# Splitting weight pieces with the low part one tile later, and re-spacing the copy, read-back and product of the DMA-transposed attention tiles

## Chip, cores and metric

One core of one Trainium2 chip runs the program. The metric is the device time of one launch in microseconds (us). The chip draws TensorE's clock from a gate: the profile gives the granted clock of a stretch as a share of full speed.

## What is computed

An attention with a mask by hashing, then a mixture of four experts, all in float32:

```python
q_bits = einsum("bhsd,dk->bhsk", q, proj) > 0        # likewise k_bits; b=2, h=8, s=768, d=64, k=6
mask = q_bucket[:, :, :, None] == k_bucket[:, :, None, :]
scores = where(mask, scale * q @ k.T, -1e9)
attn = softmax(scores) @ v                           # per batch and head
x = attn, heads side by side                         # (1536, 512)
p = domain_probs / (domain_probs.sum(-1) + 1e-9)
out = sum over e of p[:, e] * (relu(x @ w1[e]) @ w2[e])   # w1 (4, 512, 1024), w2 (4, 1024, 512)
```

## The kernel before

**Arithmetic.** Matmuls are made of rounded operands in pairs: a high part (the rounded value) and a low part (the rest), and three products (high·high, high·low, low·high) stand for one float32 product. Each operand needs a copy that rounds it (ScalarE or VectorE) and a subtraction that gives the low part (VectorE or GpSimd).

**Three stages.** First comes the attention of batch 0. Then the experts of batch 0 run interleaved with the attention of batch 1. Last come the experts of batch 1 in another form (`moe_fast`), without attention beside them. A loop at the end of the file mixes two Python generators: `moe` gives one tile of matmuls after another, and `attention` is advanced whenever its estimated cost has fallen behind the experts' by the ratio `ATT_PACE * n_att / n_moe`. Everything is written in program order, and each engine executes its own instructions in that order; nothing reorders them.

**Attention.** The work is a sequence of steps, one for each tile of 128 queries by 768 keys (six to a head). A step `i` runs the operations of `ORDER`, letter by letter, each for the tile that lies its lag behind: S, the scores (four matmuls `sps`, and their minimum on VectorE); E, the exponential on ScalarE; N and R, the row sums, which go to DRAM and come back broadcast; P, the preparation of the next head (`prep_head`), the split of v and loads. The softmax weights must then be transposed. In the first nine heads TensorE does it (T). In the last seven heads of batch 1 (`light`) it goes by DMA, two tiles (a group) at a time: X transposes blocks of 32 by 32 on VectorE and writes them to DRAM (`scr`), Y reads them back in another order (four DMAs into `ptlo`), H rounds them on ScalarE (`pthi`, line 450) and takes the low part on GpSimd (`ptlo`, line 451), V multiplies both by v (`pv`, line 461): six matmuls that read `pthi` (part 0), then six that read `ptlo` (part 1), and ScalarE and VectorE add the halves up (`xtmp`, `xraw`). There are 21 such groups. Before, both parts of V follow each other at once in the step eight behind.

**Experts.** A unit has eight tiles of the first layer (`mps`, lines 677 to 679, twelve matmuls of 384 columns; ScalarE writes `hh`, VectorE `hl`) and six of the second (lines 640 to 642, twelve matmuls of 512 columns; VectorE adds to `acc`). Weights come in loads of two pieces (`ws`, line 602, two buffers). `split_w` yields once a piece: VectorE casts the high part (line 613), GpSimd takes the low part (line 614), and behind every second piece the next load is issued. One `yield` is used up behind each tile of the layer before the one that needs the weights, and in the first stage behind every `W_STEP`-th attention operation.

**Queues.** All DMAs are issued by SyncE, in program order. A load of `ws` that waits for a buffer holds back all DMAs that are written behind it.

Of the kernel before, what the change touches and what calls it, by code (L numbers as in the profile page):

```python
# [31 lines left out]
WC = 2  # L32
N_WARM = 16
WARM = (2, 4)
FIRST = 2
W_STEP = 24
PREP_AT = 0
ORDER = "TXVSENRPHY"
LIGHT_FROM = 9
LAG_VL = 8  # L40
DRAIN = 1000
LAG_X = 3
LAG_Y = 4
# [4 lines left out]
def tile_lsh_attention__then__domain_moe(  # L48
# [206 lines left out]
    def prep_head(b, h):  # L255
        tqk = loaded.pop((0, b, h))
        q1, al, ah, k2 = stack_tiles(b, h)
        ps = big("tps")
        for c in range(NT):
            nc.tensor.transpose(  # L260
                ps[:, c // 3, (c % 3) * P : (c % 3 + 1) * P], tqk[:, c].rearrange("p a d -> p (a d)"), ident
            )
        src = ps[:, :, :NH]
        nc.scalar.activation(two(ah), src, ACTF.Copy, scale=qk_scale)
        nc.vector.scalar_tensor_tensor(
            out=two(al), in0=src, scalar=qk_scale, in1=two(ah.bitcast(F32)), op0=ALU.mult, op1=ALU.subtract
        )
        nc.sync.dma_start(out=q1[0:D].bitcast(F32), in_=ah[0:D].bitcast(F32))
        nc.sync.dma_start(out=q1[D:P].bitcast(F32), in_=ah[0:D].bitcast(F32))
        nc.sync.dma_start(out=k2[0:D].bitcast(F32), in_=ah[D:P].bitcast(F32))  # L270
        yield 654
        ps = big("hps")
        for j, (w, a) in enumerate(((phi, ah), (plo, ah), (phi, al))):
            for i in range(2):
                sl = slice(i * NH, (i + 1) * NH)
                nc.tensor.matmul(ps[:MKE, i, :NH], w, a[:, sl], start=j == 0, stop=j == 2)
        nc.sync.dma_start(out=ah[0:D].bitcast(F32), in_=al[D:P].bitcast(F32))
        nc.scalar.activation(
            two(k2[D:MKE]), ps[D:MKE, :, :NH], ACTF.Sign, bias=sgn_bias[D:MKE], scale=SGN_SCALE
        )  # L280
        yield 978
        nc.gpsimd.tensor_scalar(
            out=al[D:MKE],
            in0=k2[D:MKE].bitcast(F32),
            scalar1=1.0,
            scalar2=bit_mul[D:MKE],
            op0=ALU.add,
            op1=ALU.mult,
        )
        nc.sync.dma_start(out=k2[MQ:MQE].bitcast(F32), in_=al[MK:MKE].bitcast(F32))  # L290
        yield 0
# [218 lines left out]
    def attention():  # L510
        n = len(seq)
        prep = [iter(())]

        def stage_light(f, j):
            if 0 <= j < n and light(*seq[j][:2]) and j % G == G - 1:
                b, h, t = seq[j]
                f(b, h, t // G)

        def do(op, i):
            if op == "N":  # L520
                j = i - LAG_N
                if 0 <= j < n and j % G == G - 1:
                    b, h, t = seq[j]
                    stage_n(b, h, t // G)
            elif op == "R":
                j = i - LAG_R
                if 0 <= j < n and j % G == G - 1:
                    b, h, t = seq[j]
                    stage_r(b, h, t // G)
            elif op == "T":  # L530
                j = i - LAG_T
                if 0 <= j < n and not light(*seq[j][:2]):
                    stage_t(*seq[j])
                    return 654
            elif op == "X":
                stage_light(stage_x, i - LAG_X)
            elif op == "H":
                stage_light(stage_h, i - LAG_H)
            elif op == "Y":
                stage_light(stage_y, i - LAG_Y)  # L540
            elif op == "S":
                if i < n:
                    b, h, t = seq[i]
                    if t == 0:
                        x = hseq.index((b, h))
                        prep[0] = prep_head(*hseq[x + 1]) if x + 1 < len(hseq) else iter(())
                    stage_s(b, h, t)
                    return 652
                return DRAIN
            elif op == "V":  # L550
                c = None
                for il, lag in enumerate((LAG_V, LAG_VL)):
                    for part in range(G):
                        j = i - lag - part * (not il)
                        if 0 <= j < n and j % G == G - 1 and light(*seq[j][:2]) == bool(il):
                            b, h, t = seq[j]
                            stage_v(b, h, t // G, part)
                            if part == G - 1 and h == H - 1 and t == NT - 1:
                                done_b[b] = True
                            c = 654 + (c or 0)  # L560
                return c
            elif op == "E":
                j = i - LAG_E
                if 0 <= j < n:
                    stage_e(*seq[j])
            elif op == "P":
                if i < n:
                    b, h, t = seq[i]
                    c = next(prep[0], None) if t >= PREP_AT else None
                    x = hseq.index((b, h))  # L570
                    if t == QK_AT and x + 2 < len(hseq):
                        load_qk(*hseq[x + 2])
                    if t == 4:
                        split_v(b, h)
                        if x + 2 < len(hseq):
                            load_v(*hseq[x + 2])
                    return c
            return None

        for i in range(n + max(LAG_V, LAG_VL) + G + 1):  # L580
            for op in ORDER:
                c = do(op, i)
                if c is not None:
                    yield c
# [20 lines left out]
    def split_w(g, i):  # L605
        n = ("w1", "w2")[i]
        hi = wp.tile([P, KD, HALF], F32R, tag=n + "hi", name=n + "hi")
        lo = wp.tile([P, KD, HALF], F32R, tag=n + "lo", name=n + "lo")
        wts[g, i] = (hi, lo)
        for c in range(0, KD, WC):  # L610
            t = staged.pop((g, i, c))
            for o in range(WC):
                nc.vector.tensor_copy(hi[:, c + o], t[:, o])  # L613
                nc.gpsimd.tensor_tensor(  # L614
                    out=lo[:, c + o], in0=t[:, o], in1=hi[:, c + o].bitcast(F32), op=ALU.subtract
                )
                if o == WC - 1:
                    load_w()
                yield

    accs = {}

# [37 lines left out]
    def moe(b, first_u):  # L660
        for u in range(NU):
            w1hi, w1lo = wts.pop((first_u + u, 0))
            sp2 = split_w(first_u + u, 1) if first_u + u else iter(())
            hs = {}
            nxt = first_u + u + 1
            xo = None
            for s in range(NS):
                if nxt == NU and s == 1:
                    while next(att, None) is not None:
                        pass  # L670
                    xo = x_ops()
                sl = slice(s * SB, (s + 1) * SB)
                for f in range(FC):
                    fs = slice(f * P, (f + 1) * P)
                    ps = moe_ps()
                    for kk in range(KD):
                        nc.tensor.matmul(ps[:, :SB], w1hi[:, kk, fs], xhi[b, kk][:, sl], start=kk == 0, stop=False)  # L677
                        nc.tensor.matmul(ps[:, :SB], w1hi[:, kk, fs], xlo[b, kk][:, sl], start=False, stop=False)  # L678
                        nc.tensor.matmul(  # L679
                            ps[:, :SB], w1lo[:, kk, fs], xhi[b, kk][:, sl], start=False, stop=kk == KD - 1  # L680
                        )
                    hh = hp.tile([P, SB], F32R, tag=f"hh{f}", name="hh")
                    hl = hp.tile([P, SB], F32R, tag=f"hl{f}", name="hl")
                    nc.scalar.activation(hh, ps[:, :SB], ACTF.Relu)  # L684
                    nc.vector.scalar_tensor_tensor(  # L685
                        out=hl, in0=ps[:, :SB], scalar=0.0, in1=hh.bitcast(F32), op0=ALU.max, op1=ALU.subtract
                    )
                    hs[s, f] = (hh, hl)
                    if s == 0:
                        next(sp2, 0)  # L690
                    yield 1960
                    if xo is not None and (s, f) >= (1, 1):
                        next(xo, 0)
            for _ in xo or ():
                pass
            yield from second_layer(b, u, first_u, hs, wts.pop((first_u + u, 1)))

# [257 lines left out]
```

## Time and profile before

| | before |
|---|---|
| time, median of 3 runs | 810.42 us (810.42 to 812.13) |
| time of the profiled execution | 812.0 us |
| its span (first to last instruction) | 810.3 us |
| mean granted TensorE clock | 0.971 |
| busy in the span: TensorE, VectorE, ScalarE, GpSimd | 756.5, 506.2, 362.3, 339.1 us |
| DMA moved, mean rate | 95.49 MB, 118 GB/s |

TensorE is busy for 93% of the span. The first stage ends near 160 us, the DMA-transposed groups run from about 205 to 492 us, and the experts of batch 1 begin near 555 us. The profile is read by asking where in these stages TensorE stands still or is slow, and which instruction it then waits for.

### The profile page before, as it was taken

What the parts mean: (1) busy time and instruction counts of PE and PEld (TensorE: products, weight loads), DVE (VectorE), ACT (ScalarE), POOL (GpSimd) and SP (SyncE); (2) the same over time, 40 slices, a digit from 0 to 9 for tenths busy, and PEclk for the clock granted to TensorE, in tenths of its full rate; (3) what the DMA queues carried; (4) which work ended last, traced back from release to release, by engine and by line L of the source; (5) the groups of instructions that cost most, each with busy time, mean ns of one, the idle gap of its engine ahead of it and who ended that gap; (6) DMA issues with size and microseconds to landing.
All of it is one profiled execution on the core that took longest, in us unless ns stands there. A gap on an engine that the chain in (4) does not pass through costs nothing. (4 is left out here: it accounts for less than half of the span.)

```text
span 810.3 us, 11425 instructions
## 1 busy us (share of the span) xinstructions
PE 756.5 (93%) x4090; PEld 684.9 (85%) x4090; DVE 506.2 (62%) x957; ACT 362.3 (45%) x731; POOL 339.1 (42%) x290
## 2 busy tenths in 40 slices
PE   7899999999889899998887888999999999999998
PEld 6889889998878879888777777888899898898896
DVE  4899999755546447474555322378765756756753
ACT  4999999643434334433434211043343343433430
POOL 1232532613555446465446343375443433423520
PEclk8999999999999899999999798999999999999999
DMA  3545535425756755875276321114211211302202
GB/s 95 148 111 126 118 98 150 128 62 178 202 172 167 229 153 161 231 216 183 81 215 201 120 69 53 52 53 157 78 53 59 98 53 53 104 28 77 83 23 78
DMA packets 71953, 95.49 MB, mean 118 GB/s; under 512 B 31396, under 2 KB 47268, under 8 KB 71896
## 3 DMA queue, kind: packets, MB, share of 16 engines
q1 hardware_dynamic: 71896, 94.76, 39.9%
q8 instruction: 32, 0.52, 0.3%
q14 instruction: 25, 0.20, 0.1%
HBM read 62.68 MB, written 19.71 MB: 102 GB/s over the span
## 5 line engine op out<-in xcount | busy, mean ns | idle before, releaser
L640 PE MATMUL mps<-w2hi,hh 128*128 128x512 f32 x384 | 153.7, 400 | 0.6 <-DVE acc L648 0.4
L642 PE MATMUL mps<-w2hi,hl 128*128 128x512 f32 x384 | 153.1, 399 | 0.0
L641 PE MATMUL mps<-w2lo,hh 128*128 128x512 f32 x384 | 152.7, 398 | 0.0
L648 DVE SCALAR_TENSOR_TENSOR acc<-mps,pe,acc 128x512 f32<-128x512 f32 x84 | 62.9, 748 | 90.2 <-PE mps L642 88.8
L365 ACT ACTIVATE p<-p,nb 128x768 f32<-128x768 f32 x96 | 89.5, 932 | 14.0 <-DVE p L349 13.3
L816 POOL TENSOR_TENSOR w2lo<-ws,w2hi 128x512 fp32r<-128x512 f32 x32 | 45.8, 1452 | 114.9 <-ACT w2hi L815 114.9
L349 DVE TENSOR_SCALAR_CACHE_REDUCE p<-sps 128x768 f32<-128x768 f32 x96 | 90.3, 941 | 4.8 <-PE sps L344 4.3
L677 PE MATMUL mps<-xs,w1hi 128*128 128x384 f32 x256 | 90.0, 352 | 0.5 <-DVE hl L685 0.5
L640 PEld LDWEIGHTS mps<-w2hi,hh 128*128 128x128 f32 x384 | 73.9, 192 | 18.2 <-ACT hh L844 2.8
L678 PE MATMUL mps<-xs,w1hi 128*128 128x384 f32 x256 | 89.2, 349 | 0.0
L642 PEld LDWEIGHTS mps<-w2hi,hl 128*128 128x128 f32 x384 | 73.7, 192 | 18.0 <-DVE hl L845 2.4
L679 PE MATMUL mps<-xs,w1lo 128*128 128x384 f32 x256 | 88.9, 347 | 0.0
L685 DVE SCALAR_TENSOR_TENSOR hl<-mps,hh 128x384 fp32r<-128x384 f32 x64 | 35.6, 556 | 84.0 <-ACT hh L684 83.9
L451 POOL TENSOR_TENSOR ptlo<-ptlo,pthi 128x768 fp32r<-128x768 f32 x42 | 77.0, 1854 | 26.1 <-ACT pthi L450 14.7
L641 PEld LDWEIGHTS mps<-w2lo,hh 128*128 128x128 f32 x384 | 73.7, 192 | 13.8
L684 ACT ACTIVATE hh<-mps 128x384 fp32r<-128x384 f32 x64 | 31.4, 490 | 120.3 <-PE mps L679 120.2
L461 PE MATMUL pv<-ptlo,vv 128*128 128x256 f32 x288 | 49.3, 310 | 37.5 <-POOL ptlo L451 37.5
L614 POOL TENSOR_TENSOR w1lo<-ws,w1hi 128x512 fp32r<-128x512 f32 x32 | 41.3, 1291 | 102.3 <-DVE w1hi L613 54.8
L461 PEld LDWEIGHTS pv<-ptlo,vv 128*128 128x128 f32 x288 | 40.2, 202 | 41.4 <-POOL ptlo L451 41.3
L614 POOL TENSOR_TENSOR w2lo<-ws,w2hi 128x512 fp32r<-128x512 f32 x32 | 41.2, 1289 | 67.2 <-DVE w2hi L613 27.6
L410 DVE TENSOR_TENSOR ptlo<-ptps,pthi 128x384 fp32r<-128x384 f32 x108 | 54.5, 546 | 7.5 <-ACT pthi L409 7.3
L481 ACT ACTIVATE xtmp<-pv 64x256 f32<-64x256 f32 x48 | 18.2, 378 | 90.9 <-PE pv L461 90.3
(134 smaller groups left out, 1607.4 us busy)
## 6 DMA issues: line engine op xcount, KB each, us to landing
ws<-in_moe_w_dram SPq DMA_DIRECT2D x64, 512.0 KB
scr<-t SPq DMA_DIRECT2D x21, 768.0 KB
ptlo<-scr SPq DMA_DIRECT2D x84, 192.0 KB
q<-ah SPq DMA_DIRECT2D x30, 192.0 KB
tv<-in_v_dram SPq DMA_DIRECT2D x16, 192.0 KB
rdb<-row SPq DMA_DIRECT2D x48, 64.0 KB
out_dram<-acc SPq DMA_DIRECT2D x12, 256.0 KB
tqk<-in_q_dram SPq DMA_DIRECT2D x15, 192.0 KB
```

What stands on the lines that cost most here:

```text
L349: nc.vector.tensor_scalar(out=two(pt), in0=ps[:, :, :NH], scalar1=MASKED, scalar2=MASKED, op0=ALU.min, op1=ALU.min, accum_out=nb,)
L365: nc.scalar.activation(pt, pt, ACTF.Exp, bias=nb, scale=-1.0, accum_out=dens[b, h, g][:, o : o + 1])
L451: nc.gpsimd.tensor_tensor(out=fl[:, sl], in0=px[:, sl], in1=fh[:, sl].bitcast(F32), op=ALU.subtract)
L461: nc.tensor.matmul(ps[:, :GN].rearrange("p (a q) -> p a q", q=32) if light(b, h) else ps[:, :GN], vv[:, c], pts[b, h, g][part][:, c], star ...
L614: nc.gpsimd.tensor_tensor(out=lo[:, c + o], in0=t[:, o], in1=hi[:, c + o].bitcast(F32), op=ALU.subtract)
L640: nc.tensor.matmul(ps, hh[:, ts], w2hi[:, f], start=f == 0, stop=False)
L641: nc.tensor.matmul(ps, hh[:, ts], w2lo[:, f], start=False, stop=False)
L642: nc.tensor.matmul(ps, hl[:, ts], w2hi[:, f], start=False, stop=f == FC - 1)
L648: nc.vector.scalar_tensor_tensor(out=accs[b, tt], in0=ps, scalar=pcol, in1=accs[b, tt], op0=ALU.mult, op1=ALU.add)
L677: nc.tensor.matmul(ps[:, :SB], w1hi[:, kk, fs], xhi[b, kk][:, sl], start=kk == 0, stop=False)
L678: nc.tensor.matmul(ps[:, :SB], w1hi[:, kk, fs], xlo[b, kk][:, sl], start=False, stop=False)
L679: nc.tensor.matmul(ps[:, :SB], w1lo[:, kk, fs], xhi[b, kk][:, sl], start=False, stop=kk == KD - 1)
```

## The change

- `split_w` yields seven times instead of four. The low part of a piece is issued one yield behind its high part, and ahead of the next piece's high part; the loads are issued at the fifth and the seventh yield, two yields behind the last low part that read the buffer.
- In `moe` the split of w2 is advanced behind all eight tiles of the first layer, not only behind the first four; what is left is used up at the layer's end. `W_STEP` is 12 instead of 24.
- In `ORDER`, H stands near the front of a step, Y right behind E, and N and R behind Y.
- For DMA-transposed tiles, part 0 of V runs seven steps behind and part 1 eight, where both ran eight steps behind. `LAG_VL` also enters `n_att`, which falls from 87668 to 86668 units.
- For batch 1 (but its first head), `prep_head` yields once more ahead of the GpSimd instruction that makes the mask bits (`al`) and the DMA behind it.

```diff
-W_STEP = 24
+W_STEP = 12
-ORDER = "TXVSENRPHY"
+ORDER = "THXVSEYNRP"
-LAG_VL = 8
+LAG_VL = 7
...
         yield 978
+        if b and h:
+            yield 0
         nc.gpsimd.tensor_scalar(
...
-                        j = i - lag - part * (not il)
+                        j = i - lag - part
...
-        for c in range(0, KD, WC):
-            t = staged.pop((g, i, c))
-            for o in range(WC):
-                nc.vector.tensor_copy(hi[:, c + o], t[:, o])
+        st = {}
+        for c in range(KD + 3):
+            if 1 <= c <= KD:
                 nc.gpsimd.tensor_tensor(
-                    out=lo[:, c + o], in0=t[:, o], in1=hi[:, c + o].bitcast(F32), op=ALU.subtract
+                    out=lo[:, c - 1], in0=st[c - 1], in1=hi[:, c - 1].bitcast(F32), op=ALU.subtract
                 )
-                if o == WC - 1:
-                    load_w()
-                yield
+            if c < KD:
+                if c % WC == 0:
+                    t = staged.pop((g, i, c))
+                st[c] = t[:, c % WC]
+                nc.vector.tensor_copy(hi[:, c], st[c])
+            if c in (WC + 2, KD + 2):
+                load_w()
+            yield
...
-                    if s == 0:
-                        next(sp2, 0)
+                    next(sp2, 0)
...
+            for _ in sp2:
+                pass
```

The order of instructions at three places follows. In the changed kernel the lines that were 450, 451, 461, 602, 613 and 614 are 452, 453, 463, 604, 622 and 615.

TensorE, one group's product in the middle of the second stage, before (`pv` is the product, `mps` an expert tile):

```order
L679 MATMUL mps<-xs_119,w1lo 128x384
L677 MATMUL mps<-xs_120,w1hi 128x384
L678 MATMUL mps<-xs_120,w1hi 128x384
L679 MATMUL mps<-xs_120,w1lo 128x384
L461 MATMUL pv<-pthi,vv 128x256 x6
L461 MATMUL pv<-ptlo,vv 128x256 x6
L677 MATMUL mps<-xs_117,w1hi 128x384
L678 MATMUL mps<-xs_117,w1hi 128x384
```

The same engine with the change, around the second half of a group's product:

```order
L647 MATMUL mps<-w2lo,hh 128x512
L648 MATMUL mps<-w2hi,hl 128x512
L344 MATMUL sps<-ah,q_3692 128x384 x2
L346 MATMUL sps<-k_3695,al 128x384 x2
L463 MATMUL pv<-ptlo,vv 128x256 x6
L646 MATMUL mps<-w2hi,hh 128x512
L647 MATMUL mps<-w2lo,hh 128x512
```

The six matmuls that read `pthi` no longer stand directly ahead of the six that read `ptlo`: an expert tile of twelve rows and the scores of a step lie between them.

GpSimd, the 18th to the 20th group, before (`ptlo` is the low part of the transposed tile, `w1lo` and `w2lo` those of weight pieces):

```order
L451 TENSOR_TENSOR ptlo<-ptlo,pthi 128x768 x2
L614 TENSOR_TENSOR w1lo<-ws,w1hi 128x512
L451 TENSOR_TENSOR ptlo<-ptlo,pthi 128x768 x2
L614 TENSOR_TENSOR w1lo<-ws,w1hi 128x512
L495 TENSOR_TENSOR xraw<-xraw,rdb 128x256
L614 TENSOR_TENSOR w1lo<-ws,w1hi 128x512 x2
L451 TENSOR_TENSOR ptlo<-ptlo,pthi 128x768 x2
```

The same groups with the change:

```order
L453 TENSOR_TENSOR ptlo<-ptlo,pthi 128x768 x2
L615 TENSOR_TENSOR w2lo<-ws,w2hi 128x512
L453 TENSOR_TENSOR ptlo<-ptlo,pthi 128x768 x2
L615 TENSOR_TENSOR w1lo<-ws,w1hi 128x512 x2
L453 TENSOR_TENSOR ptlo<-ptlo,pthi 128x768 x2
```

A weight piece still stands ahead of the pair of the 19th group, but it is now one whose high part was cast behind the tile before; the piece whose cast stands behind the latest tile comes after the pair.

SyncE, from one group's read-back to the write of the group after the next, before (`scr` is the DRAM buffer, `ws` a weight load):

```order
L437 DMA ptlo<-scr 32x4x384 x4
L428 DMA scr<-t_3376 128x1536
L381 DMA row<-rt 4x32 x2
L290 DMA k_3264<-al 12x768
L602 DMA ws<-in_moe_w_dram 128x2x512
L388 DMA rdb<-row 64x256
L437 DMA ptlo<-scr 32x4x384 x4
L428 DMA scr<-t_3493 128x1536
```

The same head with the change:

```order
L430 DMA scr<-t_3374 128x1536
L604 DMA ws<-in_moe_w_dram 128x2x512
L383 DMA row<-rt 4x32 x2
L439 DMA ptlo<-scr 32x4x384 x4
L390 DMA rdb<-row 64x256
L292 DMA k_3284<-al 12x768
L430 DMA scr<-t_3509 128x1536
```

The read-back now stands ahead of the broadcast of the row sums (`rdb`) and of the mask bits (`k<-al`). A weight load can still stand ahead of it.

## Rows read from the trace of the kernel before

**Rows 1.** Windows: stretch, its length, busy us of each engine, clock, DMA.

```profile
20.00:200.00 180.00, 174.22 (x1177) 161.23 (x1178) 151.08 (x354) 138.87 (x309) 62.43 (x79) 1.00 0.48 124
200.00:500.00 300.00, 261.16 (x1339) 239.20 (x1338) 149.82 (x288) 108.43 (x207) 155.10 (x115) 0.93 0.57 165
500.00:811.00 311.00, 305.87 (x1516) 272.18 (x1514) 195.55 (x285) 106.40 (x202) 118.02 (x77) 1.00 0.20 70
```

**Rows 2.** Waits, 200 to 500 us: us in total, times, longest.

```profile
PE pv L461 <- POOL ptlo L451: 37.5, 18, 3.5
```

**Rows 3.** Timeline around one stall: start, us, engine, line, tiles, [idle before <-releaser].

```profile
450.99 1.58 ACT L450 ACTIVATE pthi<-ptlo 128x768 fp32r<-128x768 f32 x2
...
453.98 0.42 DVE L613 CAST w1hi<-ws 128x512 fp32r<-128x512 f32 x1
...
454.53 1.29 POOL L614 TENSOR_TENSOR w1lo<-ws,w1hi 128x512 fp32r<-128x512 f32 x1 [10.79 <-issue]
...
455.78 3.76 POOL L451 TENSOR_TENSOR ptlo<-ptlo,pthi 128x768 fp32r<-128x768 f32 x2
455.83 0.88 PE L461 MATMUL pv<-pthi,vv 128*128 128x256 f32 x6
...
456.70 1.18 DVE L613 CAST w1hi<-ws 128x512 fp32r<-128x512 f32 x1
...
459.60 1.65 PE L461 MATMUL pv<-ptlo,vv 128*128 128x256 f32 x6 [2.88 <-POOL ptlo L451]
```

**Rows 4.** Timeline of TensorE behind another stall, in a first-layer tile.

```profile
443.80 0.99 PE L461 MATMUL pv<-ptlo,vv 128*128 128x256 f32 x6 [1.94 <-POOL ptlo L451]
...
445.14 0.49 PE L677 MATMUL mps<-xs,w1hi 128*128 128x384 f32 x1
...
446.39 0.52 PE L678 MATMUL mps<-xs,w1hi 128*128 128x384 f32 x1
446.71 0.52 PE L679 MATMUL mps<-xs,w1lo 128*128 128x384 f32 x1
...
448.61 0.34 PE L679 MATMUL mps<-xs,w1lo 128*128 128x384 f32 x1
...
449.31 0.33 PE L677 MATMUL mps<-xs,w1hi 128*128 128x384 f32 x1
449.48 0.33 PE L678 MATMUL mps<-xs,w1hi 128*128 128x384 f32 x1
```

**Rows 5.** Groups by line, 200 to 500 us: busy, mean ns, idle before.

```profile
L451 POOL TENSOR_TENSOR ptlo<-ptlo,pthi 128x768 fp32r<-128x768 f32 x42 | 77.0, 1854 | 26.1 <-ACT pthi L450 14.7 <-DMA ptlo<-scr 11.4
...
L424 DVE STREAM_TRANSPOSE t<-p 128x768 f32<-128x768 f32 x38 | 34.7, 952 | 0.0
...
L450 ACT ACTIVATE pthi<-ptlo 128x768 fp32r<-128x768 f32 x42 | 33.1, 836 | 7.0 <-DMA ptlo<-scr 6.9
```

**Rows 6.** Timeline of SyncE, 333 to 352 us: issues of DMAs.

```profile
334.28 2.07 SPq L437 DMA_DIRECT2D ptlo<-scr  x4
...
346.63 0.40 SPq L602 DMA_DIRECT2D ws<-in_moe_w_dram  x1
...
348.08 1.93 SPq L437 DMA_DIRECT2D ptlo<-scr  x4
```

**Rows 7.** Timeline of GpSimd, same stretch.

```profile
345.30 1.30 POOL L614 TENSOR_TENSOR w1lo<-ws,w1hi 128x512 fp32r<-128x512 f32 x1 [1.28 <-DVE w1hi L613]
```

**Rows 8.** Timeline of SyncE, a write to DRAM and the read behind it.

```profile
417.47 0.34 SPq L428 DMA_DIRECT2D scr<-t  x1
...
424.68 1.87 SPq L437 DMA_DIRECT2D ptlo<-scr  x4
```

**Rows 9.** Timeline of ScalarE, 333 to 352 us: a copy that waited for the read.

```profile
340.88 1.58 ACT L450 ACTIVATE pthi<-ptlo 128x768 fp32r<-128x768 f32 x2 [0.89 <-DMA ptlo<-scr]
```

**Rows 10.** Line 613, the cast of a weight piece: shortest, median, longest ns.

```profile
L613 DVE CAST w1hi<-ws x32: 407/417/2032, 71.2 to 516.5; 128x512 fp32r<-128x512 f32 x32
```

**Rows 11.** Waits of the whole span for weight loads, in the last stage.

```profile
ACT w1hi L771 <- DMA ws<-in_moe_w_dram: 8.5, 7, 1.3
```

## The prediction

> **What bounds the kernel now.** Read the windows first. From 20 to 200 us TensorE is busy for 174.2 of 180 us, and from 500 us to the end for 305.9 of 310 us of span, both at a granted clock of 1.00; from 200 to 500 us it is busy for 261.2 of 300 us, at 0.93 [rows 1]. So only the middle stage, where the DMA-transposed attention runs beside the experts, holds time that an order of instructions can free: 300 − 261.2 = 38.8 us of idle TensorE, and (1 − 0.93) × 300 = 21 us of half clock. The other engines are not the bound there: VectorE is busy for 149.8 us, GpSimd for 155.1, ScalarE for 108.4 [rows 1].
>
> Then the waits of that stage: 37.5 of the 38.8 us are one wait, the second half of the product (`pv`) for GpSimd's low part (`ptlo`, line 451), 18 times among 21 groups, 2.1 us each [rows 2].
>
> Then one such wait on the timeline. ScalarE has rounded the tile by 452.6 us, its first half even at 451.8. GpSimd could start then, but the low part of a weight piece stands ahead in its queue, and this waits for a cast that VectorE makes only at 453.98, since the cast stands behind the addition of the expert tile. So the weight piece runs at 454.53, the two subtractions of the tile from 455.78 to 459.54; TensorE had asked for them at 456.7 and stands until 459.60 [rows 3].
>
> The clock follows. Behind a stall of 1.94 us TensorE's matmuls of 384 columns fall from 0.17 us apart to 0.32 from 445.14 to about 448.6, that is 1.2 for 2.4 GHz, and then return [rows 4]. Such a fall costs 3.4 × (1 − 0.17/0.32) = 1.6 us; the 21 us are about 13 of them for 18 stalls.
>
> **The change part by part.** The order of the changed program settles the distances; I price them with durations from rows.
>
> *Copy earlier, product split.* Before, from the place of the copy (H) to the half that reads `ptlo` TensorE mostly has one expert tile, one step's scores and the first half: 12 × 0.17 = 2.0 us for a first-layer tile [rows 4], four score matmuls at the same pace 0.7, the half 0.9 [rows 3], together 3.6 us (with a second-layer tile, by its columns 512/384 as long, 4.3). The chain needs 0.8 us for the first copy and 2 × 1.85 for the subtractions [rows 5], 4.5 us, and up to 1.3 more for a weight piece ahead and whatever this waits for. That misses 3.6 by 1 us and more, which is what is seen. With the change three to five expert tiles, up to two steps' scores and two halves lie between: at least 3 × 2.0 + 2 × 0.7 + 2 × 0.9 = 9.2 us. The chain with a weight piece and the two copies is 1.7 + 3.7 + 1.3 = 6.7. The stall should go in every group whose read-back is in time: −37.5 us.
>
> *Low part one tile behind.* The piece that now stands ahead of the subtractions had its cast a tile earlier, so it does not wait for VectorE. Its work is the same, 1.3 us a piece. What it would cost to keep it in the old place is in the 6.7 us above; the 9.2 would cover that too, so the two edits secure the same gain and are not added.
>
> *Loads later.* Before, a load of weights waits on SyncE for the low part, and the read-back stands behind it: the load at 346.63 waited for GpSimd's piece that ended at 346.60, and the read went out at 348.08 [rows 6, 7]. With the load two yields later its buffer is free when SyncE arrives. This shortens the way to the read and adds nothing; its danger is the last rival below.
>
> *Read-back to copy.* This distance shrinks, from about three tiles to one or two, so the whole way has to be checked: blocks transposed 1.9 us [rows 5], written and ready to be read within 7.2 (417.47 to 424.68) [rows 8], read within 6.6 (334.28 to 340.88, where the copy waited for it) [rows 6, 9], copied 1.7, and 1 us for the VectorE work ahead: 18.4 us at most. In ten groups with a head's preparation in between, TensorE has over 25 us from X to the first half by the same paces. In the eleven others it has five to seven tiles and up to four steps' scores, 18 to 22 us. Below, a miss is excluded for most; above, a miss in all eleven would cost what the stalls cost now (the first rival). I take 0.7 us for each of the eleven, 8 us, nearest to the case in which the ends just meet.
>
> *The clock.* With the stalls gone the stage should run as the others do, at 1.00: −21 us (by the rounding of 0.93, 19.5 to 22.5).
>
> *The rest at nothing:* seven yields for four and `W_STEP` 12 move the same eight casts and pieces of the first stage, where VectorE is busy for 151 of 180 us [rows 1]; if that cover is gone a cast costs 0.42. The mask bits a step later leave three steps of over 5 us before their scores. Broadcasts behind the read-back are used two steps on. The ratio of the mix moves by 1%, and the work of TensorE is the same.
>
> Sum: 812.0 (the profiled execution, 1.7 of it outside the span) − 37.5 − 21 + 8 = 761.5. The median of the runs is 1.6 below that execution, so 760. With no residue it is 752, and the whole 38.8 and 22.5 give a floor of 749.
>
> **The rivals.**
>
> *The read-back arrives late.* Then ScalarE's copy waits for the DMA, and TensorE for `pthi` instead of `ptlo`. For it: the stage moves its data at 165 GB/s [rows 1] and will move the same bytes in a fifth less time; one copy waits already [rows 9]. Against it: 18.4 is a sum of worst cases. If the eleven tight groups each stall as now, with a fall of the clock: 11 × (2.1 + 1.6) = 41 us instead of 8, 793.
>
> *Casts held by GpSimd.* GpSimd's subtractions now start while a cast of the same tile is due. A cast beside line 451 took 1.18 us at 456.70 [rows 3], the longest 2.03 against a median of 0.42 [rows 10]. If one cast in each of 21 groups is held for 1.6 us and this reaches TensorE, 34 us come back and there is no other residue: 812.0 − 58.5 + 34 − 1.6 = 786. Against it: VectorE has 150 idle us in the stage [rows 1]. The Trainium skill (SBUF — State Buffer, section "SBUF: two separate sides") says that VectorE's two-port instructions and GpSimd take one pair of ports by an exclusive lock for a whole instruction. By that rule the cast waits out a subtraction, and the trace agrees: 2.03 is less than 0.42 + 1.85.
>
> *The clock does not follow.* Smaller stalls remain that still lower it: 812.0 − 37.5 − 1.6 = 773.
>
> *One wait for another, in full.* The order moves, and the time stays near 810, within 0.2% (1.6 us, which is also about what a measurement of this kernel can tell from no change).
>
> *Slower: weights late.* A load goes out two tiles later and the cast that needs it blocks VectorE's queue, with the score minima and additions behind it, on which TensorE's PSUM buffers depend. About 22 loads fall in the stage. The gain of 58.5 us is used up when each is late by 2.7 us beyond what TensorE has in hand. Late by 4 us each: 812.0 − 58.5 + 88 − 1.6 = 840. Against it: two to four tiles with attention between, over 7 us, still lie between a load and its cast, and where loads are waited for today, in the last stage, it is 8.5/7 = 1.2 us [rows 11].
>
> **How the numbers follow.** Forecast 0.62 (749 to 772), read-back late 0.15 (772 to 793), casts held 0.08 (786), clock not following 0.07 (773), same 0.03, weights late 0.05. Faster by over 0.2%: 0.62 + 0.15 + 0.08 + 0.07 = 0.92; same 0.03; slower 0.05. From 750 to 786 lie the forecast, the clock case, about half of the late read-back and the held casts, 0.84; much narrower would leave out the last two.
>
> **What would show it.** Right: the middle stage is some 50 us shorter at a clock of 0.99 or 1.00, `pv` waits for `ptlo` for under 5 us in all, and SyncE's loads no longer wait for GpSimd. Late read-back: waits of `pv` for `pthi`, and of `pthi` for the DMA, of over 10 us. Held casts: their mean far above 0.6 us and TensorE waiting for VectorE. Weights late: VectorE waiting for `ws`. The prediction is wrong if the stage keeps more than 25 us of idle or slow clock.

## The result, and the profile after

The change makes the kernel 7.3% faster: 752.26 us (median of 4 runs, 751.21 to 752.96) against 811.02 us of before (median of 4), a ratio of 0.9273 with a 95% interval of 0.9257 to 0.9289. Forecast were 760.0 us, in a range of 750 to 786. The execution of the change that was profiled took 751.21 us, with a span of 749.5; the profiled execution of before took 812.0, with a span of 810.3. The difference is 60.8 us, and TensorE's row of the page splits it:

```profile
PE 733.6 (98%) x4090; PEld 668.7 (89%) x4090; DVE 517.3 (69%) x957; ACT 363.2 (48%) x731; POOL 342.7 (46%) x290
```

TensorE executes the same 4090 instructions. It was idle for 810.3 − 756.5 = 53.8 us, and is now for 749.5 − 733.6 = 15.9 us: 37.9 us less. It was busy for 756.5 us, and is now for 733.6: 22.9 us less for the same matmuls. 37.9 + 22.9 = 60.8. Nearly all of the 22.9 is the clock: its mean over the span rose from 0.971 to 0.997, and (1 − 0.971) × 810.3 − (1 − 0.997) × 749.5 = 21 us.

The windows of the kernel after, in the columns of [rows 1], say where:

```profile
20.00:200.00 180.00, 172.80 (x1168) 159.75 (x1169) 149.55 (x352) 139.23 (x307) 65.84 (x81) 1.00 0.47 122
200.00:500.00 300.00, 299.35 (x1641) 277.52 (x1641) 198.67 (x335) 124.60 (x235) 185.07 (x130) 1.00 0.63 181
...
500.00:750.00 250.00, 245.74 (x1218) 218.58 (x1216) 158.73 (x240) 89.56 (x174) 88.12 (x60) 1.00 0.20 69
```

All of it comes from the middle stage. The experts' first-layer tiles begin at 149.8 us in the kernel before and at 150.1 now, and the last stage, from the first matmul of `moe_fast` to the end, takes 253 us in both (557.4 to 810.3, and 496.6 to 749.5); what lies between took 407.6 us and takes 346.5. Between 200 and 500 us TensorE was busy for 261.16 us at a clock of 0.93, and now for 299.35 at 1.00, with 1641 of its instructions in the stretch for 1339. The first stage lost a little: between 20 and 200 us TensorE is busy for 172.80 us, for 174.22 before.

The waits in the kernel after, over the whole span (waiting engine, tile and line, the releaser, us in total, times, longest): TensorE's three largest, ScalarE's for the read-back, and SyncE's for GpSimd's low parts of the weights:

```profile
PE hps L276 <- DVE al L265: 2.8, 7, 0.7
PE sps L346 <- POOL vv L305: 1.7, 1, 1.7
PE warm L131 <- POOL qk_scale L122: 1.4, 1, 1.4
...
ACT pthi L452 <- DMA ptlo<-scr: 15.6, 6, 4.7
...
SPq L604 <- POOL w2lo L615: 31.4, 6, 11.9
SPq L604 <- POOL w1lo L615: 18.2, 3, 12.8
```

SyncE's in the kernel before:

```profile
SPq L602 <- POOL w1lo L614: 82.2, 16, 13.0
SPq L602 <- POOL w2lo L614: 81.4, 15, 12.9
```

TensorE's wait of `pv` for `ptlo` [rows 2] is gone, and none for `pthi` has come in its place. ScalarE does wait for the read, 15.6 us in six groups, for 6.9 us before [rows 5]. A load held SyncE for a low part 31 times before, 163.6 us in all, and does so 9 times now, 49.6 us. In the chain of work that ended last TensorE itself is now 82% of the span. The 38% on the page of before is no measure against it, since that chain is followed back only to 443.7 us.

```profile
PE 82%; DVE 8%; ACT 3%; POOL 3%; DMA 2%; issue 1%; SPq 0%; POOLq 0%; DVEq 0%; ACTq 0%
```

Two groups on the timeline of the kernel after (columns as in [rows 3]), first one whose read-back came late, so that ScalarE waited for it, then one without that:

```profile
319.82 1.17 SPq L383 DMA_DIRECT2D row<-rt  x2
323.68 1.73 SPq L439 DMA_DIRECT2D ptlo<-scr  x4
...
329.27 1.58 ACT L452 ACTIVATE pthi<-ptlo 128x768 fp32r<-128x768 f32 x2 [2.20 <-DMA ptlo<-scr]
...
331.47 3.85 POOL L453 TENSOR_TENSOR ptlo<-ptlo,pthi 128x768 fp32r<-128x768 f32 x2
...
333.29 0.88 PE L463 MATMUL pv<-pthi,vv 128*128 128x256 f32 x6
...
342.15 0.84 PEld L463 LDWEIGHTS pv<-ptlo,vv 128*128 128x128 f32 x6
...
387.79 1.56 ACT L452 ACTIVATE pthi<-ptlo 128x768 fp32r<-128x768 f32 x2
...
389.49 0.91 PE L463 MATMUL pv<-pthi,vv 128*128 128x256 f32 x6
...
395.14 0.88 PE L463 MATMUL pv<-ptlo,vv 128*128 128x256 f32 x6
```

In the first the copy is done at 330.85, and TensorE reads its result at 333.29 without a wait; GpSimd is done at 335.32, and the second half loads its first weights at 342.15, 6.8 us later. In the stall of [rows 3] GpSimd's work ended 0.06 us before TensorE went on. Over the 21 groups the second half now starts between 2.7 and 9.5 us behind the end of the subtractions. The first half follows its input more closely: 0.1 to 9.0 us behind the end of the copy, and in two groups 0.1, the second of those shown among them, where the copy ends at 389.35. So no product waits for its input, but the copy has little to spare in some groups.

### The profile page after: what moved, and what is told of

Its sections match the earlier page's. It is cut to its first block, busy times and chain, and to the rows that moved or that the text cites. A ratio compares the mean times of both kernels' runs of the same rounds, so it can differ in the third digit from the quotient of the medians.

```text
span 749.5 us, 11443 instructions
## 1 busy us (share of the span) xinstructions
PE 733.6 (98%) x4090; PEld 668.7 (89%) x4090; DVE 517.3 (69%) x957; ACT 363.2 (48%) x731; POOL 342.7 (46%) x290
## 4 chain that ended last, share of the span: by engine, by line
PE 82%; DVE 8%; ACT 3%; POOL 3%; DMA 2%; issue 1%; SPq 0%; POOLq 0%; DVEq 0%; ACTq 0%
PE mps L646 11%; PE mps L648 11%; PE mps L647 11%; PE mps L683 6%; PE mps L685 6%; PE mps L684 6%; PE pv L463 6%; PE sps L346 3%; PE sps L344 2%; PE mps L841 2%; PE mps L837 2%; PE mps L840 2%; DVE p L351 2%; PE hps L276 2%; PE pa L840 2%; PE pa L837 1%
## 5 line engine op out<-in xcount | busy, mean ns | idle before, releaser
L646 PE MATMUL mps<-w2hi,hh 128*128 128x512 f32 x384 | 151.6, 395 | 0.8 <-DVE acc L654 0.4
L648 PE MATMUL mps<-w2hi,hl 128*128 128x512 f32 x384 | 151.0, 393 | 0.0
L647 PE MATMUL mps<-w2lo,hh 128*128 128x512 f32 x384 | 150.0, 391 | 0.0
L646 PEld LDWEIGHTS mps<-w2hi,hh 128*128 128x128 f32 x384 | 72.1, 188 | 17.8 <-ACT hh L851 2.8
L648 PEld LDWEIGHTS mps<-w2hi,hl 128*128 128x128 f32 x384 | 72.1, 188 | 17.5 <-DVE hl L852 2.4
L683 PE MATMUL mps<-xs,w1hi 128*128 128x384 f32 x256 | 86.7, 338 | 0.5 <-DVE hl L691 0.5
L685 PE MATMUL mps<-xs,w1lo 128*128 128x384 f32 x256 | 86.2, 337 | 0.0
L684 PE MATMUL mps<-xs,w1hi 128*128 128x384 f32 x256 | 86.0, 336 | 0.0
L615 POOL TENSOR_TENSOR w1lo<-ws,w1hi 128x512 fp32r<-128x512 f32 x32 | 42.0, 1319 | 40.0 <-DVE w1hi L622 38.3
L346 PE MATMUL sps<-k,al 76*128 76x384 f32 x192 | 50.5, 343 | 3.3 <-POOL vv L305 1.7
L344 PE MATMUL sps<-ah,q 128*128 128x384 f32 x192 | 50.6, 344 | 1.9 <-DVE ah L244 1.1
L782 POOL TENSOR_TENSOR w1lo<-ws,w1hi 128x512 fp32r<-128x512 f32 x24 | 35.9, 1496 | 34.0 <-ACT w1hi L778 34.0
```

What stands on the lines that cost most here:

```text
L344: nc.tensor.matmul(ps[:, i, :NH], q1[:, sl], k1[:, i * NH : (i + 1) * NH], start=True, stop=False)
L346: nc.tensor.matmul(ps[:, i, :NH], q2[0:MQE, sl], k2[0:MQE, i * NH : (i + 1) * NH], start=False, stop=True)
L615: nc.gpsimd.tensor_tensor(out=lo[:, c - 1], in0=st[c - 1], in1=hi[:, c - 1].bitcast(F32), op=ALU.subtract)
L646: nc.tensor.matmul(ps, hh[:, ts], w2hi[:, f], start=f == 0, stop=False)
L647: nc.tensor.matmul(ps, hh[:, ts], w2lo[:, f], start=False, stop=False)
L648: nc.tensor.matmul(ps, hl[:, ts], w2hi[:, f], start=False, stop=f == FC - 1)
```

## The experiments

The prediction names three edits that could carry the gain (order and product, low part, loads), and gives all of it to the first. The runs undo them one by one and do them alone. Each time is a median, each ratio is to the kernel before on the same chip with its 95% interval. The changed kernel itself stands at 0.9273 and, measured again beside the last three runs, at 0.9281.

### Both sides by themselves

**The split of the weight pieces undone, the attention as in the change:** the low part straight behind its high part, the load straight behind the second of them.

```diff
-W_STEP = 12
+W_STEP = 24
...
-        for c in range(KD + 3):
+        for c in range(0, KD, WC):
+            t = staged.pop((g, i, c))
+            for o in range(WC):
+                nc.vector.tensor_copy(hi[:, c + o], t[:, o])
...
+                    out=lo[:, c + o], in0=t[:, o], in1=hi[:, c + o].bitcast(F32), op=ALU.subtract
...
+                if o == WC - 1:
+                    load_w()
+                yield
...
-                    next(sp2, 0)
+                    if s == 0:
+                        next(sp2, 0)
```

> Of the changed kernel, the weight split alone as before: four yields, each low part straight behind its high part, loads behind them, W_STEP 24. Theory 'distance' (TensorE stalls by what the chain from ScalarE's copy to the second half of the product needs beyond the TensorE work written between them): that work stays at 9.2 us or more, the chain with a piece that waits for its cast is 6 to 7 us, so hardly a stall comes back: 752 to 758 us, pv waiting for ptlo under 3 us in all. Rival 'queue' (what counts is that GpSimd's piece and SyncE's load no longer wait): most stalls come back, 785 us or more, pv waiting for over 15 us.

Measured: 780.16 us (779.26 to 784.26), ratio 0.9640 [0.9587, 0.9693]. Half of the gain is gone, the time lies between the two expectations, and the wait is a new one. TensorE's and ScalarE's waits of this run, and SyncE's:

```profile
PE pv L463 <- ACT pthi L452: 16.9, 8, 3.7
ACT pthi L452 <- DMA ptlo<-scr: 54.1, 10, 14.0
SPq L604 <- POOL w1lo L616: 70.3, 16, 11.5
SPq L604 <- POOL w2lo L616: 58.3, 15, 11.4
```

No second half waits for `ptlo`: the distance from the copy to the subtraction's reader is long enough even with the old weight pieces. It is the first half that waits for the copy, the copy for the read, and the read in SyncE's queue, as one place on the timeline of this run shows:

```profile
256.22 0.39 SPq L604 DMA_DIRECT2D ws<-in_moe_w_dram  x1
256.71 1.83 SPq L439 DMA_DIRECT2D ptlo<-scr  x4
...
263.66 1.58 ACT L452 ACTIVATE pthi<-ptlo 128x768 fp32r<-128x768 f32 x2 [4.68 <-DMA ptlo<-scr]
...
265.29 0.98 PE L463 MATMUL pv<-pthi,vv 128*128 128x256 f32 x6 [2.43 <-ACT pthi L452]
```

SyncE had nothing to issue after 251 us, stood at the load until GpSimd's second low part ended at 256.18, issued it, and the read right behind. In the kernel after, the same group's read goes out at 249.62, behind loads at 241.16 and 243.72, and the copy runs at 257.40 without a wait. So beside the new attention the split is worth 27.9 us (780.16 − 752.26), by a way that the prediction had seen and priced at nothing: SyncE's queue.

**The attention undone, the split as in the change:**

```diff
-ORDER = "THXVSEYNRP"
+ORDER = "TXVSENRPHY"
-LAG_VL = 7
+LAG_VL = 8
...
-                        j = i - lag - part
+                        j = i - lag - part * (not il)
```

> Of the changed kernel, the attention steps alone as before: ORDER, LAG_VL 8, both halves of the product in one step; the new weight split stays. 'Distance': between copy and second half lie 1.5 to 6 us of TensorE work again, mostly 3.6, against 4.5 us for the copy and two subtractions, 5.8 with a piece ahead: stalls of 1 to 2 us in most of 21 groups, 15 to 35 us in all, clock falls in part of them: 775 to 800 us. 'Queue': the stalls are gone or under 5 us, 752 to 760 us.

Measured: 783.16 us (781.92 to 784.54), ratio 0.9668 [0.9619, 0.9717]. The old wait is there, in 12 groups for 18 and about half as long in all:

```profile
PE pv L463 <- POOL ptlo L453: 20.2, 12, 2.2
```

Each side by itself is worth about half of the gain, and by different waits.

### The attention's parts

**Both halves of the product in one step, all else as in the change** (the last two edits of the diff above, without `ORDER`):

> Of the changed kernel, both halves of the product in one step again, eight behind; the copy keeps its new place. 'Distance': the second half stands where it stood, 9.4 us or more behind the copy, so nothing changes: 750 to 756 us; splitting the product is worth nothing by itself. A rival, that the split is what removes the stall (TensorE gets other work between the halves): 765 us or more, pv waiting for ptlo again.

Measured: 750.99 us (750.75 to 751.76), ratio 0.9274 [0.9220, 0.9327]: no difference. That the product is cut in two steps earns nothing here.

**The old `ORDER`, the product still cut in two:**

```diff
-ORDER = "THXVSEYNRP"
+ORDER = "TXVSENRPHY"
```

> Of the changed kernel, ORDER alone as before, the product split over two steps as in the change. 'Distance': the first half now stands directly behind the copy with no TensorE work between, and waits for two copies of 0.84 us and the relu ahead of them, about 2 us in each of 21 groups, over 30 us in all, now put down to pthi; the second half has 3.6 us or more against 3.7 for the subtractions and waits a little too. With clock falls 795 to 815 us. Rival 'queue': the order matters little, 752 to 765 us.

Measured: 797.95 us (795.12 to 799.72), ratio 0.9847 [0.9793, 0.9900]. The first half, now a step earlier, waits for the copy in 12 groups:

```profile
PE pv L463 <- ACT pthi L452: 29.2, 12, 3.0
```

So of the attention's edits it is the new order that pays, 45.7 us by its own undoing (797.95 − 752.26). That is more than the 30.9 us of the whole attention undone: a product cut in two without the earlier copy costs more than it saves.

**The read-back moved behind N, R and P in its step,** which is behind the broadcast of the row sums in SyncE's queue; all else as in the change:

```diff
-ORDER = "THXVSEYNRP"
+ORDER = "THXVSENRPY"
```

> Of the changed kernel, the read-back (Y) at the end of its step, behind the row sums' broadcast, as before. The margin of the changed kernel (ScalarE's copy waited for reads 15.6 us in all, TensorE not at all) is then used by the broadcast, which waits for the row sums to land: 'load' (reads in time are what counts): 752 to 765 us, pv waiting for pthi up to 8 us. If the place of the read in the queue is without effect: 750 to 753 us.

Measured: 781.77 us (780.32 to 782.59), ratio 0.9648 [0.9597, 0.9698]. The mechanism was expected, the size was not: 29.5 us. The broadcast waits for the row sums' own write (38.6 us in this run, 10.1 in the change), and the read stands behind it:

```profile
PE pv L463 <- ACT pthi L452: 20.8, 6, 4.8
ACT pthi L452 <- DMA ptlo<-scr: 53.2, 11, 7.9
SPq L390 <- DMA row<-rt: 38.6, 27, 4.6
```

### The split's parts

**Loads early:** as the change, with the low part one tile behind, but each load straight behind the last low part that reads its buffer.

```diff
-            if c in (WC + 2, KD + 2):
+            if c in (WC, KD):
```

> Of the changed kernel, the loads straight behind the last low part that frees their buffer (third and fifth yield); the low parts stay one tile behind their high parts. 'Load': SyncE is held again, but for less, since the low part does not wait for the latest cast: 755 to 775 us, with pv waiting for pthi. 'Low part': 750 to 755 us.

Measured: 778.03 us (777.57 to 778.57), ratio 0.9604 [0.9554, 0.9653]. This one condition is worth 25.8 us, nearly all that the whole split is worth (27.9), and more than was expected. SyncE's waits for low parts are back at 65.8 and 51.9 us, ScalarE's for the read at 50.4 in 14 groups, TensorE's for the copy at 15.6 in 7.

**Only the loads late:** the low part straight behind its high part again, the loads two yields behind it.

```diff
-        for c in range(KD + 3):
-            if 1 <= c <= KD:
-                nc.gpsimd.tensor_tensor(
-                    out=lo[:, c - 1], in0=st[c - 1], in1=hi[:, c - 1].bitcast(F32), op=ALU.subtract
-                )
+        for c in range(KD + 2):
...
-            if c in (WC + 2, KD + 2):
+                nc.gpsimd.tensor_tensor(
+                    out=lo[:, c], in0=st[c], in1=hi[:, c].bitcast(F32), op=ALU.subtract
+                )
+            if c in (WC + 1, KD + 1):
```

> Of the changed kernel, the low part straight behind its high part again, in the same yield; the loads stay two yields behind the low part that frees their buffer. The run with the whole old split gave 780 us with pv waiting for pthi and pthi for the read-back DMA. Theory 'load' (what brought those 28 us back is SyncE held by a load in front of the read-back): loads stay late, so the reads are in time: 750 to 757 us, pv waiting for pthi under 3 us. Rival 'low part' (the piece that waits for its cast ahead of the subtractions costs it): 770 us or more.

Measured: 754.01 us (753.87 to 754.10), ratio 0.9307 [0.9250, 0.9365], with no wait of `pv`. The low part one tile behind is worth about 2 us beside the new order.

**The same, under the old order and product:** here the low part stands behind its high part, the loads come late, and the attention is that of before. More than the loads still differs from the kernel before: `W_STEP` 12, the advance of w2's split behind all eight tiles, and the empty yield stay as in the change.

> The kernel before (its order, its product 8 half steps behind, both halves in one step), with one thing of the change: the loads of the next weight piece two tiles later, the low part still straight behind its high part. Theory 'distance': in the old order the copy and GpSimd's second half lie too close to the product, whatever the loads do: 795 to 812 us, with products waiting for the second half of the copied tile. Rival 'loads alone': the 27 us that the new split gave under the old order came from the late loads, and the time is that of the run with the attention undone, 781 to 787 us.

Measured: 818.98 us (814.89 to 822.41), ratio 1.0098 [1.0065, 1.0131]: slower than before, and outside both expectations, though on the side of the first. Against the run with the attention undone (783.16) the place of the low part differs, and with it the load goes out one yield earlier and the split has one yield less. Reads hardly count in either run (ScalarE waits 0.6 us for them here, 1.1 there), and `pv` waits for `ptlo` 40.0 us here and 20.2 there. So most of the 36 us between them is put down to the place of the low part; it was not moved by itself. One group of each on the timeline shows why. First this run, with the loads late alone:

```profile
342.25 1.57 ACT L452 ACTIVATE pthi<-ptlo 128x768 fp32r<-128x768 f32 x2
...
344.99 1.29 POOL L619 TENSOR_TENSOR w1lo<-ws,w1hi 128x512 fp32r<-128x512 f32 x1 [5.01 <-issue]
...
347.16 0.42 DVE L618 CAST w1hi<-ws 128x512 fp32r<-128x512 f32 x1
...
347.66 1.30 POOL L619 TENSOR_TENSOR w1lo<-ws,w1hi 128x512 fp32r<-128x512 f32 x1 [1.38 <-DVE w1hi L618]
...
350.06 3.77 POOL L453 TENSOR_TENSOR ptlo<-ptlo,pthi 128x768 fp32r<-128x768 f32 x2
...
353.88 0.99 PE L463 MATMUL pv<-ptlo,vv 128*128 128x256 f32 x6 [2.55 <-POOL ptlo L453]
```

Then the run with the low part one tile behind, the same group:

```profile
331.73 1.58 ACT L452 ACTIVATE pthi<-ptlo 128x768 fp32r<-128x768 f32 x2 [0.33 <-DMA ptlo<-scr]
...
334.09 1.29 POOL L615 TENSOR_TENSOR w1lo<-ws,w1hi 128x512 fp32r<-128x512 f32 x1 [5.06 <-DMA scr<-t]
...
336.48 3.71 POOL L453 TENSOR_TENSOR ptlo<-ptlo,pthi 128x768 fp32r<-128x768 f32 x2
...
340.27 0.96 PE L463 MATMUL pv<-ptlo,vv 128*128 128x256 f32 x6
```

With the low part straight behind, GpSimd must take a second piece first, whose cast comes at 347.16, behind a further expert tile; the subtractions start 7.81 us behind the start of the copy, for 4.75 us in the other run, and TensorE waits for 2.55 us there and not here. Late loads could give nothing in this run: ScalarE waits 0.6 us in all for a read. Of the 8 us by which it is slower than before, 2.5 are longer waits for `ptlo` (40.0 us for 37.5) and 2.6 lie in the first stage, where TensorE is busy for 171.59 of 180 us, for 174.22 before; the rest was not followed.

**The split undone and the product together:** the edits of the first run and of the third.

> The whole old weight split, with the copy in its new place and both halves of the product eight steps behind. The first half then stands 8.5 us or more behind the copy, not 3.6, and 21 us or more behind the block transposes, not 18.4. 'Load': a read-back that is late by 2 to 4 us no longer reaches TensorE: 750 to 760 us. If the 28 us come instead from GpSimd or from the weights themselves, they stay: 775 us or more.

Measured: 794.78 us (791.25 to 795.75), ratio 0.9802 [0.9748, 0.9857]. The theory 'load' gave 750 to 760 us and is wrong here; the time lies in the rival's range, but TensorE waits 3.2 us in all for `ptlo` and never for weights, so the rival's causes do not bring it. With the product in one step the first half is read later, so a late read was to be covered. But ScalarE waits for the read in 20 of 21 groups, 111.8 us, and while it waits nothing behind the copy in its queue runs. On the timeline:

```profile
443.06 1.58 ACT L452 ACTIVATE pthi<-ptlo 128x768 fp32r<-128x768 f32 x2 [9.19 <-DMA ptlo<-scr]
444.66 0.38 ACT L483 ACTIVATE xtmp<-pv 64x256 f32<-64x256 f32 x1
...
445.07 0.42 DVE L488 TENSOR_TENSOR xraw<-pv,xtmp 64x256 f32<-64x256 f32 x1 [11.39 <-ACT xtmp L483]
...
445.54 0.79 PE L642 MATMUL mps<-w2hi,hh 128*128 128x512 f32 x1 [4.22 <-DVE xraw L488]
```

ScalarE stands for 9.19 us at the copy; the copy out of an earlier product's PSUM (`xtmp`) stands behind it, VectorE's sum behind that, and TensorE waits 4.22 us in an expert tile that has nothing to do with the read. A late read so reaches TensorE by ScalarE's queue, even where the product could wait. Of TensorE's 28.9 idle us between 200 and 500 us only 8.3 are waits of `pv`. Counted in the order of the program at the matmul paces of the prediction, this kernel has a median of 3.4 us of TensorE's work between the read and the copy, for some 6 in the change. That alone does not do it: the run with only the product together has the same 3.4 us, and there, with the new split, ScalarE waits 28.1 us in 9 groups and the time is 750.99. The short distance and the load in front of the read make the many waits together.

### Small things

**Without the empty yield between heads** (`if b and h: yield 0` taken out; it is `prep_head`'s, not that of the weight pieces, which the expectation names):

> The changed kernel without the empty yield that the generator of the weight pieces makes between heads. Theory 'not on the path': the empty step only moves work of the cores' other engines, and 751 to 754 us are left, with no wait of a product for the transposed tile. Rival: without it the additions of the row groups reach GpSimd earlier, GpSimd waits for a transfer ahead of the subtractions of the low parts, and TensorE waits for GpSimd or for the copy: 756 to 765 us.

Measured: 750.50 us (749.96 to 751.94), ratio 0.9259 [0.9231, 0.9288]. The empty yield is worth nothing.

**A candidate:** the product together, `W_STEP` 8 for 12, the empty yield for every head.

```diff
-W_STEP = 12
+W_STEP = 8
-LAG_VL = 7
+LAG_VL = 8
...
-        if b and h:
-            yield 0
+        yield 0
...
-                        j = i - lag - part
+                        j = i - lag - part * (not il)
```

> A candidate: the changed kernel with both halves of the product in one step, the weight pieces' steps begun at 8 in place of 24, and the empty yield for every head. If the 2.9 us in which TensorE waits for GpSimd near the end of the first third, where GpSimd is held by a transfer of the row groups, go with it: 747 to 751 us. If they only move: 751 to 754 us, as the changed kernel.

Measured: 756.82 us (755.59 to 759.72), ratio 0.9339 [0.9306, 0.9373]: 4 us slower than the change on the same chip, and outside both expectations. The first stage lost it (TensorE busy for 169.32 of 180 us): its scores wait for the mask bits' DMA, 4.5 us in 4 waits, and the wait for GpSimd is 3.9 us for 2.9. The name of the new wait points to the empty yield, behind which those bits are made; it was not tried by itself.

**The change once more,** beside the last three:

> The changed kernel once more, beside the three others on the same chip: 751 to 753 us.

Measured: 752.73 us (751.49 to 752.99), ratio 0.9281 [0.9253, 0.9310]. No variant beats it by more than the intervals.

## Why the prediction was right, and where it was not

**What bounds the kernel** was read rightly. The 58.5 us that the waits and the clock of one stage showed are what came: 37.9 us of idle and 22.9 us of busy time, for 37.5 and 21 in the sum. The middle stage is 61 us shorter, for the 50 that the prediction named as a sign.

**Copy earlier.** The −37.5 us came in full. That the new order brings it is shown: undoing it alone costs 45.7 us. The prediction wrote "copy earlier, product split" as one term; the split half of it is worth nothing.

**Low part one tile behind.** "The two edits secure the same gain and are not added" holds: the place of the low part is worth about 2 us beside the new order, and most of 36 us under the old. With the split alone, under the old order, nearly half of the gain comes (783.16 us). The reason given, that the piece ahead of the subtractions waits for VectorE's cast, is what the two timelines show.

**Loads later** is the step that failed. The prediction said that this edit "shortens the way to the read and adds nothing". It is worth 25.8 us. The waits of the loads in SyncE's queue were seen [rows 6, 7], but they cost nothing in the kernel before, whose copies start 6.6 to 19.5 us behind the issue of their reads (ScalarE waited 6.9 us in all [rows 5]), and so were priced at nothing in the kernel after too. There the new order has taken that room away: the copies start 5.4 to 12.0 us behind it. A cover was used up by one edit, and another edit had to replace it; the sum should have named the loads as a condition of the first term. That the time still came out right is luck in this point: both edits are in the same change, so the mistake does not show in the sum. Nor did the sign that SyncE's loads no longer wait for GpSimd come in full, since 9 waits are left. What shows when the loads are not late is the rival "the read-back arrives late", by its own signs, waits of `pv` for `pthi` and of `pthi` for the DMA: 778 to 782 us in the three runs that undo the late loads or the read's place, for the 793 that all eleven tight groups would have given. One way of it was not in the rival: ScalarE's queue, by which a late copy also holds what is behind it.

**Read-back to copy, +8 us,** is the term that was mis-sized: it measured 0. The prediction had 18.4 us of need against 18 to 22 of room in eleven groups. ScalarE does wait in six groups, 15.6 us in all, but TensorE in none; the closest first half runs 0.1 us behind its copy. The ends did just meet, on the good side of it, and 752 us, which the prediction gave for no residue, is what was measured.

**The clock** followed, some 21 us by its mean, as forecast. In the kernel before it fell nine times between 200 and 500 us, to half for 41 us in all; the prediction's 13 falls of 3.4 us are much the same loss, in other pieces. In the runs that kept some of the waits the loss came back in part, in step with TensorE's idle time. For each the idle time of TensorE from 200 to 500 us, the granted clock there, what these two would cost (idle + (1 − clock) × 300 us), and the time above the 752.26 us of the change:

| run | idle, us | clock | sum, us | measured, us |
|---|---|---|---|---|
| old attention, loads late | 41.3 | 0.93 | 62 | 66.7 |
| before | 38.8 | 0.93 | 60 | 58.8 |
| old order, product cut | 29.4 | 0.95 | 44 | 45.7 |
| split undone, product together | 28.9 | 0.95 | 44 | 42.5 |
| attention undone | 21.5 | 0.98 | 28 | 30.9 |
| read-back last | 20.8 | 0.96 | 33 | 29.5 |
| split undone | 16.9 | 0.97 | 26 | 27.9 |
| loads early | 15.7 | 0.98 | 22 | 25.8 |
| the change | 0.7 | 1.00 | 1 | 0 |

Within some 5 us the two terms account for every one of them. Nearly all of the idle time is waits of `pv`, but for the run with the split undone and the product together. The rival "the clock does not follow" did not come: in the change, and in the variants without such waits, the granted clock of the stretch is 1.00.

**Casts held by GpSimd** happens, more often than before, and costs TensorE nothing. The casts of the kernel after (shortest, median, longest ns):

```profile
L622 DVE CAST w1hi<-ws x32: 407/419/2072, 62.3 to 455.7; 128x512 fp32r<-128x512 f32 x32
L622 DVE CAST w2hi<-ws x32: 398/420/1844, 123.5 to 469.8; 128x512 fp32r<-128x512 f32 x32
```

The longest is 2.07 us for 2.03 before [rows 10], and the median is the same, but neither tells how many are held. The means do (busy us, mean ns), before and after:

```profile
L613 DVE CAST w1hi<-ws 128x512 fp32r<-128x512 f32 x32 | 18.1, 565 | 0.0
L613 DVE CAST w2hi<-ws 128x512 fp32r<-128x512 f32 x32 | 17.3, 546 | 0.1
...
L622 DVE CAST w1hi<-ws 128x512 fp32r<-128x512 f32 x32 | 24.6, 768 | 0.0
L622 DVE CAST w2hi<-ws 128x512 fp32r<-128x512 f32 x32 | 22.2, 694 | 0.0
```

Of the 64 casts 21 take longer than 0.6 us, for 9 before, and together they take 11 us more, which is all that VectorE's busy time grew by (506.2 to 517.3 us). VectorE is busy for 198.67 of 300 us in the stage, and TensorE never waits for a cast, so the second of the prediction's two signs is missing. The Trainium skill (SBUF — State Buffer, section "SBUF: two separate sides") has VectorE wait out a whole instruction of GpSimd at the ports that they share; the trace agrees, since 2.07 us is less than a cast and a subtraction together, 0.42 + 1.88. **Weights late** did not come: no wait for `ws` stands among VectorE's in the middle stage. **The rest at nothing** holds for the empty yield (750.50 without it) and was 1.4 us off in the first stage.

## What to carry to other kernels

When an edit moves one step of a chain earlier, the room that it gains behind the step is taken from the way ahead of it: price the whole chain again (here write, read-back, copy, subtraction, product), and what stands in the issuing queue in front of each transfer, since a wait that was free before the edit may be on the path after it. Where several edits come together, ask of each whether it adds a gain, secures the same one, or is the condition of another: here the place of the copy brings the time, the late loads and the read's early place keep it, and each of the others can be left out by itself. An engine that stands at one late operand holds everything behind it in its queue, so a late read can surface as a wait for something else.

## What the runs showed of the hardware

Two things stand out. The clock's cost went with TensorE's idle time in every run, by the table some 0.3 to 0.6 us for one of idling (21 us for 38.8 before, 6 for 21.5 with the attention undone), though no single wait of `pv` was longer than 5.4 us, and none in that last run longer than 2.2; a short wait that comes back in many groups costs more than its own length. And a load that SyncE cannot issue yet costs most by what stands behind it: in the run with the loads early, its 118 us of standing at loads (65.8 + 51.9) came out as 50.4 us of ScalarE waiting for a read and 15.6 us of TensorE waiting for the copy; with the loads two yields later it is 49.6, 15.6 and none.
